# One core, fused attention and two dense blocks: a tile's scores begin one round later, and the next batch's v is fetched ten rounds later

## The chip, the cores and the metric

The kernel runs on one core of one Trainium2 chip. The metric is device time in microseconds of that core. Three runs of the kernel before took 867.61, 865.63 and 867.61 us, median 867.61. In what follows PE is the matrix engine (TensorE), PEld its weight loads, ACT the scalar engine, DVE the vector engine, POOL GpSimd, and SP the engine that issues the DMAs.

## What is computed

Attention with the heads mixed before and after the softmax, then two dense blocks. The change touches only the attention, for 4 batches, 12 heads, 448 rows and a head size of 64:

```python
scores = scale * np.matmul(q, k.transpose(0, 1, 3, 2))
scores = np.einsum('bhij,hg->bgij', scores, w_pre)      # mix heads
scores = scores - np.max(scores, axis=-1, keepdims=True)
attn = np.exp(scores)
attn = attn / (np.sum(attn, axis=-1, keepdims=True) + 1e-09)
attn = np.einsum('bhij,hg->bgij', attn, w_post)         # mix heads again
return np.matmul(attn, v)
```

Its result `x` goes through `_moe_ref` (a gated block with `w_in`, `w_sg`, `w_out`) and `_moe2_ref` (a block with `w_theta`, `w_tok_r`, `w_tok_i`, `w_ch`), which are left out here.

## The kernel before

**Tiles and rounds.** Each batch's 448 rows are cut into four tiles of 120, 120, 120 and 88 rows. A tile is worked off in rounds of two blocks of 10 rows (all 12 heads of 10 rows fill 120 partitions), so the four tiles of a batch have 6, 6, 6 and 5 rounds, 23 in a batch and 92 in all. Round r of the main loop is not one block's work from end to end but a slice of a software pipeline, written out by hand: `relayout(r + 4)`, `postmix(r)`, `premix(r + 2)` with its `rowmax` and `expo`, and parts of other tiles that tables of round numbers place there.

**The steps that matter.**

- `scores(b, t, c)` (L113 to L137): eight matmuls (L130) for the head pair c of a tile, into `psA`, a pool with one buffer (L66), then one ACT copy (L137) into the tile's `s`, a pool with two buffers (L61). A tile needs six of these, c = 0 to 5. So tile T's first copy writes the buffer of tile T - 2, and has to wait until all of that tile's relayouts have read it.
- `relayout(r)` (L142 to L148): two DMAs, SBUF to SBUF, that bring two blocks of `s` into `blk`, with heads on partitions.
- `premix(r)` (L150 to L156): eight matmuls from `blk` into two `psB` buffers, all there are of them (L74). `rowmax` (L162, DVE) and `expo` (L170, ACT) read them, so the premix of the next round can write them when these are done.
- `postmix(r)` (L192 to L207): 56 small matmuls (L201, L206), and two copies of the result into `at` (L218).
- `attn_v(b, t, c)` (L229 to L247): 20 matmuls (L242, L246) of the finished tile with v, six per tile, in the rounds of the tile after it.
- `load_k`, `load_q`, `load_v`: DMAs from SP. `vt` holds the v of two batches in turn.

**What sets the order.** Each engine works in the order in which the main loop writes instructions. In a round it is: relayout; the table `early` (DMAs); postmix; the copies into `at`; the tables `front` and `mid`; premix, rowmax, expo; the tables `work` and `late`. `units(T)` (L277) gives the rounds in which the six `scores` of tile T stand, spread evenly from `lo` to `hi`; the first in a round goes to `front` (ahead of the premix), a second one in the same round to `work` (after it, and before `attn_v`). `load_q` stands three rounds ahead of the first score, and the six `load_k` of the next batch stand in the rounds of the fourth tile's scores. `extra` is the decoding of a weight (L476 to L511) for the dense block, in steps on ACT, DVE and POOL in some of the rounds.

In what follows a round with no score is called an empty round, one with two scores a double round.

Of the kernel before, what the change touches and what calls it, by code (L numbers as in the profile page):

```python
# [28 lines left out]
LR, LQ = 4, 2  # L29
# [5 lines left out]
def attention(tc, nc, io, xT, B, extra, tail):  # L35
# [9 lines left out]
    tiles = [(b, t) for b in range(B) for t in range(len(TILES))]  # L45
    nt = len(tiles)
    first, last = {}, {}
# [4 lines left out]
    with ExitStack() as es:  # L52
# [219 lines left out]
        early, front, mid, work, late = {}, {}, {}, {}, {}  # L272

        def put(d, r, fn, *a):
            d.setdefault(r, []).append((fn, a))

        def units(T):  # L277
            lo, hi = first[tiles[T - 1]] - LR, first[tiles[T]] - LR - 1
            return [lo + (c * (hi - lo + 1)) // NP for c in range(NP)]

        for T in range(1, nt):
            b, t = tiles[T]
            u = units(T)
            for c in range(NP):
                put(front if u[c] not in u[:c] else work, u[c], scores, b, t, c)
            if T > 1:
                put(early, u[0] - QO, load_q, b, t)
            if t == 0:
                for c, r in enumerate(units(T - 1)):
                    put(early, r, load_k, b, c)  # L290
        for b in range(B):
            f = first[b, 0]
            for j in range(4):
                put(early, f - 14 + 3 * j if b else 1 + j, load_v, b, j)
        for T in range(nt):
            b, t = tiles[T]
            for c in range(NP):
# [815 lines left out]
def build(tc, nc, io, out):  # L1113
    with tc.manual_schedule(), ExitStack() as top:
        dram = top.enter_context(tc.tile_pool(name="scratch", bufs=1, space=bass.MemoryType.DRAM))
        xT = dram.tile([DM, B * S], F32, name="xT")
        x2T = dram.tile([DM, B * S], F32, name="x2T")
        d = Dense(tc, nc, io, xT, x2T, out)
        d.scratch(dram)
        right, left1, left2 = ExitStack(), ExitStack(), ExitStack()  # L1120
        tail, win_es, last_u, end = moe1(d, left1, right)
        th_es = moe2(d, left2, win_es, last_u, left1)
        for i in range(4):
            tail.setdefault(-2 + 2 * i, []).append(d.step)
        slots = top.enter_context(ExitStack())
        d.open_slots(slots)
        jobs = []
        for half, ks in ((1, range(KD)), (0, range(KE))):
            for k in ks:
                jobs += d.decode_tiles(io["w_in"], slice(128 * k, 128 * k + 128), HF * half, HF * half + HF,  # L1130
                                       lambda k=k, half=half: d.pieces(k, half))
        attention(tc, nc, io, xT, B, jobs, tail)
        while d.at < len(d.units):
            d.step()
        th_es.close()
        right.close()
        slots.close()
        left2.close()
# [69 lines left out]
```

## Time and profile before

| | |
|---|---|
| median of three runs | 867.61 us (865.63 to 867.61) |
| the profiled execution | 866.24 us |
| its span, first to last instruction | 864.5 us |
| attention: rounds 0 to 91 | 20 to 345 us of the span |
| PE busy | 842.7 us, 97% of the span |
| ACT busy | 493.6 us, 57% |
| DVE busy | 592.1 us, 68% |
| mean granted clock of PE | 0.996 of full speed |
| DMA moved | 142.16 MB, mean 164 GB/s |

A row of the timeline reads: start in us from the span's start, duration, engine, line, operation, result<-operands, shapes, count, and in brackets how long the engine was idle before it and what ended that. A row of the waits reads: who waited, for whom, us in total, times, longest. A row of the windows has, for one stretch, each engine's busy us, then the granted clock of PE (1.00 is 2.4 GHz, 0.50 is 1.2 GHz), the busy share of the DMA engines and GB/s. Matmuls overlap in the rows, so the time a step takes on PE is read from start to start. Line numbers are those of the kernel before.

### The profile page before, as it was taken

What the parts mean: (1) busy time and instruction counts of PE and PEld (TensorE: products, weight loads), DVE (VectorE), ACT (ScalarE), POOL (GpSimd) and SP (SyncE); (2) the same over time, 40 slices, a digit from 0 to 9 for tenths busy, and PEclk for the clock granted to TensorE, in tenths of its full rate; (3) what the DMA queues carried; (4) which work ended last, traced back from release to release, by engine and by line L of the source; (5) the groups of instructions that cost most, each with busy time, mean ns of one, the idle gap of its engine ahead of it and who ended that gap; (6) DMA issues with size and microseconds to landing.
All of it is one profiled execution on the core that took longest, in us unless ns stands there. A gap on an engine that the chain in (4) does not pass through costs nothing.

```text
span 864.5 us, 27167 instructions
## 1 busy us (share of the span) xinstructions
PE 842.7 (97%) x10984; PEld 664.9 (77%) x10984; DVE 592.1 (68%) x1364; ACT 493.6 (57%) x1106; POOL 204.6 (24%) x404
## 2 busy tenths in 40 slices
PE   7999999899989999999999999999999999999998
PEld 2465666466656666798988989898999999999997
DVE  5566676467666776879999998779784378338231
ACT  3688788579877886584845767247443155025010
POOL 0222223122222222000000000038228047306321
PEclk9999999899999999999999999999999999999999
DMA  5667657565776546551757867997611221300301
GB/s 195 212 223 227 196 180 229 179 201 172 249 202 209 177 158 167 153 159 50 247 180 240 270 196 230 351 299 230 214 38 45 83 54 31 118 19 1 118 11 64
DMA packets 108877, 142.16 MB, mean 164 GB/s; under 512 B 25680, under 2 KB 94800, under 8 KB 108752
## 3 DMA queue, kind: packets, MB, share of 16 engines
q1 hardware_dynamic: 108752, 140.42, 51.4%
q8 instruction: 87, 1.43, 0.7%
q14 instruction: 38, 0.31, 0.1%
HBM read 74.26 MB, written 27.59 MB: 118 GB/s over the span
## 4 chain that ended last, share of the span: by engine, by line
PE 91%; issue 3%; DMA 2%; DVE 2%; ACT 1%; POOL 0%; ACTq 0%; POOLq 0%; DVEq 0%; SPq 0%
PE ps L442 55%; PE psB L156 8%; PE psD L242 8%; PE psA L130 8%; PE psC L201 7%; PE psD L246 3%; DMA blk<-s 2%; PE psC L206 1%; PE ps L960 1%; DMA x<-x2T 1%; ACT s L137 0%; ACT e L170 0%; DVE s L134 0%; POOL x2s L438 0%; POOL z L438 0%
## 5 line engine op out<-in xcount | busy, mean ns | idle before, releaser
L170 ACT ACTIVATE e<-psB,nmx 128x448 f32<-128x448 f32 x180 | 112.3, 629 | 49.0 <-DVE nmx L162 47.3
L162 DVE TENSOR_REDUCE nmx<-psB 128x1 f32<-128x448 f32 x180 | 104.1, 619 | 27.9 <-PE psB L156 26.1
L442 PE MATMUL ps<-wtok,z 128*128 128x448 f32 x504 | 104.8, 368 | 0.0
L130 PE MATMUL psA<-k,q 64*64 64x448 f32 (+2 forms) x768 | 93.7, 547 | 10.1 <-ACT s L137 8.0
L242 PEld LDWEIGHTS psD<-at,v 128*64 128x64 f32 x1152 | 56.5, 137 | 60.6 <-issue 39.9
L442 PEld LDWEIGHTS ps<-wtok,z 128*128 128x128 f32 x504 | 94.6, 188 | 9.5
L156 PE MATMUL psB<-blk,kpre 64*64 64x448 f32 x720 | 97.9, 541 | 1.9 <-DMA blk<-s 1.1
L442 PE MATMUL ps<-wth,x2s 128*128 128x384 f32 x504 | 94.2, 342 | 2.4 <-POOL x2s L438 1.8
L137 ACT ACTIVATE s<-psA 124x896 f32<-124x896 f32 (+1 forms) x90 | 82.7, 919 | 24.0 <-PE psA L130 12.2
L438 POOL TENSOR_TENSOR x2s<-x,x2s 128x384 fp32r<-128x384 f32 x28 | 28.8, 1047 | 278.2 <-DMA xres<-xT 201.8
L442 PEld LDWEIGHTS ps<-wth,x2s 128*128 128x128 f32 x504 | 88.1, 188 | 4.1 <-POOL x2s L438 2.8
L442 PE MATMUL ps<-u,wch 128*128 128x448 f32 x432 | 89.9, 368 | 0.0
L442 PEld LDWEIGHTS ps<-u,wch 128*128 128x128 f32 x432 | 81.0, 188 | 8.1
L201 PE MATMUL psC<-wr,e 64*64 64x60 f32 x4320 | 83.4, 220 | 1.7 <-issue 1.1
L201 PEld LDWEIGHTS psC<-wr,e 64*64 64x64 f32 x4320 | 74.1, 136 | 8.6 <-POOL wr L188 5.3
L242 PE MATMUL psD<-at,v 128*64 128x120 f32 (+1 forms) x1152 | 77.3, 269 | 0.0
L438 POOL TENSOR_TENSOR z<-zz,z 128x384 fp32r<-128x384 f32 x56 | 63.8, 1159 | 56.4 <-ACT z L435 56.3
L435 ACT ACTIVATE u<-xres 128x448 fp32r<-128x448 f32 x24 | 13.8, 577 | 98.1 <-DVE xres L1021 98.1
L156 PEld LDWEIGHTS psB<-blk,kpre 64*64 64x64 f32 x720 | 36.7, 132 | 42.5 <-issue 19.3
L176 POOL TENSOR_SCALAR rc<-sum 128x2 f32<-128x2 f32 (+1 forms) x92 | 17.9, 195 | 210.5 <-ACT e L170 210.5
L188 POOL TENSOR_SCALAR wr<-wts,rc 128x60 f32<-128x60 f32 x180 | 54.1, 314 | 48.1 <-DVE rc L181 36.5
L442 PE MATMUL ps<-slot,x 128*128 128x512 f32 x252 | 60.1, 396 | 0.0
(111 smaller groups left out, 1437.6 us busy)
## 6 DMA issues: line engine op xcount, KB each, us to landing
blk<-s SPq DMA_DIRECT2D x176, 210.0 KB
draw<-in_w_in SPq DMA_DIRECT2D x24, 256.0 KB
k<-in_kvT SPq DMA_DIRECT2D x24, 224.0 KB
xraw<-xT SPq DMA_DIRECT2D x24, 224.0 KB
xres<-xT SPq DMA_DIRECT2D x24, 224.0 KB
x2T<-xres SPq DMA_DIRECT2D x24, 224.0 KB
xres<-x2T SPq DMA_DIRECT2D x24, 224.0 KB
out<-uu SPq DMA_DIRECT2D x24, 224.0 KB
```

Of the source, the lines that this page charges most:

```text
L130: nc.tensor.matmul(ps[e][r, :S], q[p, o + r.start:o + r.stop], k[p], start=True, stop=True)
L137: nc.scalar.activation(out=out, in_=pair[:m, :, :S], func=AF.Copy, scale=0.125)
L156: nc.tensor.matmul(ps[e][c:c + 64, :S], kpre[k, e], blk[k], start=True, stop=True)
L162: nc.vector.tensor_reduce(out=nmx[r][:, e:e + 1], in_=ps[:, :S], axis=AX.X, op=ALU.max, negate=True)
L170: nc.scalar.activation(out=x, in_=ps[:, :S], func=AF.Exp, bias=m[:, e:e + 1], accum_out=sm[:, e:e + 1])
L176: nc.gpsimd.tensor_scalar(out=rc[:, :m], in0=sm[:, :m], scalar1=1e-9, scalar2=1.0, op0=ALU.add, op1=ALU.mult)
L188: nc.gpsimd.tensor_scalar(out=w, in0=wts, scalar1=rc[:, e:e + 1], scalar2=0.0, op0=ALU.mult, op1=ALU.add)
L201: nc.tensor.matmul(pc[r][h][c:c + 64, o:o + H], x[p, 128 * jc + c:128 * jc + c + 64], w[p], start=(e == 0 and jc == 0), stop=(not two and ...
L242: nc.tensor.matmul(ps[p], v[:, jc, p], main[:, H * jc + 2 * c + i], start=(o == 0 and jc == 0), stop=False)
L246: nc.tensor.matmul(px[p] if e else ps[p, 0], v[q, 3, p], rest[q, 2 * c + i], start=(o == 0 and e == 1), stop=(o > TI))
L438: eng.tensor_tensor(out=out, in0=in_, in1=hi.bitcast(F32), op=ALU.subtract)
L442: self.nc.tensor.matmul(ps, l, r, start=(i == 0), stop=(i == len(terms) - 1))
```

## The change

```diff
         def units(T):
-            lo, hi = first[tiles[T - 1]] - LR, first[tiles[T]] - LR - 1
+            lo, hi = first[tiles[T - 1]] - LR + (T > 1), first[tiles[T]] - LR - 1
             return [lo + (c * (hi - lo + 1)) // NP for c in range(NP)]
...
             for j in range(4):
-                put(early, f - 14 + 3 * j if b else 1 + j, load_v, b, j)
+                put(early, f - 3 + 2 * j if b else 1 + j, load_v, b, j)
```

`lo` moves one round later from tile 2 on, `hi` stays. Where the tile before has six rounds, six scores stood in six rounds, 1 1 1 1 1 1, and now stand as 0 2 1 1 1 1. Where it has five (the first tile of batches 1, 2 and 3), they stood as 2 1 1 1 1 and now stand as 0 2 1 2 1. `load_q`, and the `load_k` of a batch's end, move with them. The four parts of the next batch's v stood 14, 11, 8 and 5 rounds before the batch's first round f, and now stand at f - 3, f - 1, f + 1 and f + 3; the first `attn_v` that reads it is in round f + 6.

On PE, round 38 (in batch 1's last tiles; the scores are those of the first tile of batch 2) was

```order
L206 MATMUL psC<-wr,e 64x60 x4
L130 MATMUL psA<-k,q 64x448 x2
L130 MATMUL psA<-k,q 60x448 x2
L156 MATMUL psB<-blk_136,kpre 64x448
L156 MATMUL psB<-blk_137,kpre 64x448
L156 MATMUL psB<-blk_136,kpre 64x448
L156 MATMUL psB<-blk_137,kpre 64x448
L242 MATMUL psD<-at,v 64x2x12x5 x6
```

from the end of its postmix to the start of its attn_v. In the changed kernel the same round, on PE, is

```order
L206 MATMUL psC<-wr,e 64x60 x4
L130 MATMUL psA<-k,q 64x448 x2
L130 MATMUL psA<-k,q 60x448 x2
L156 MATMUL psB<-blk_136,kpre 64x448
L156 MATMUL psB<-blk_137,kpre 64x448
L156 MATMUL psB<-blk_136,kpre 64x448
L156 MATMUL psB<-blk_137,kpre 64x448
L130 MATMUL psA<-k,q 64x448 x2
L130 MATMUL psA<-k,q 60x448 x2
L242 MATMUL psD<-at,v 64x2x12x5 x6
```

A second score now stands behind the premix and ahead of attn_v; before, this was so one round earlier, in round 37, which now has no score.

On ACT, rounds 37 and 38 (`at` is the copy after the postmix, `s` the copy of a score, `e` the two exponentials, `dp`, `dl` and `slot` belong to the decoding) were

```order
L218 COPY at<-psC 128x84x5
L137 ACTIVATE s<-psA 124x896
L484 ACTIVATE dp<-draw 128x256
L485 ACTIVATE dl<-draw 128x256
L170 ACTIVATE e,sum<-psB,nmx 128x448 x2
L137 ACTIVATE s<-psA 124x896
L218 COPY at<-psC 128x84x5
L137 ACTIVATE s<-psA 124x896
L500 ACTIVATE slot<-da 128x256
L170 ACTIVATE e,sum<-psB,nmx 128x448 x2
```

and the same two rounds on ACT, with the first row of the next one, are now

```order
L218 COPY at<-psC 128x84x5
L484 ACTIVATE dp<-draw 128x256
L485 ACTIVATE dl<-draw 128x256
L170 ACTIVATE e,sum<-psB,nmx 128x448 x2
L218 COPY at<-psC 128x84x5
L137 ACTIVATE s<-psA 124x896
L500 ACTIVATE slot<-da 128x256
L170 ACTIVATE e,sum<-psB,nmx 128x448 x2
L137 ACTIVATE s<-psA 124x896
L218 COPY at<-psC 128x84x5
```

The copy of a double round's second score stands behind both exponentials. Each tile from tile 2 on now has such a place.

On SP, the DMAs of rounds 35 to 37 (the `blk` are relayouts) were

```order
L96 DMA k<-in_kvT 128x448
L108 DMA v<-in_vN 128x768
L476 DMA draw<-in_w_in 128x512
L148 DMA blk_136<-s 120x1x448
L148 DMA blk_137<-s 120x1x448
L96 DMA k<-in_kvT 128x448
L269 DMA xT<-x 128x3x120
L148 DMA blk_138<-s 120x1x448
L148 DMA blk_139<-s 120x1x448
```

and on SP the same stretch is now

```order
L96 DMA k<-in_kvT 128x448
L476 DMA draw<-in_w_in 128x512
L148 DMA blk_136<-s 120x1x448
L148 DMA blk_137<-s 120x1x448
L96 DMA k<-in_kvT 128x448
L269 DMA xT<-x 128x3x120
L148 DMA blk_138<-s 120x1x448
L148 DMA blk_139<-s 120x1x448
```

The part of v that stood ahead of round 36's relayout (`blk_136`, `blk_137`, the last that reads the `s` of the tile two before) is gone from there.

## Rows read from the trace of the kernel before

**Rows 1.** The page: PE's busy time, share of the span and instructions

```profile
PE 842.7 (97%) x10984; PEld 664.9 (77%) x10984; DVE 592.1 (68%) x1364; ACT 493.6 (57%) x1106; POOL 204.6 (24%) x404
```

**Rows 2.** Waits of the attention stage: waiter <- releaser, total, times, longest

```profile
ACT s L137 <- DMA blk<-s: 8.9, 5, 4.1
```

**Rows 3.** Timeline, rounds 61 and 62: score, its copy, first exponential, next score

```profile
246.00 0.94 PE L130 MATMUL psA<-k,q 64*64 64x448 f32 x8
...
247.01 0.92 ACT L137 ACTIVATE s<-psA 124x896 f32<-124x896 f32 x1 [0.22 <-PE psA L130]
...
248.49 0.63 ACT L170 ACTIVATE e<-psB,nmx 128x448 f32<-128x448 f32 x1 [0.56 <-DVE nmx L162]
...
249.37 0.94 PE L130 MATMUL psA<-k,q 64*64 64x448 f32 x8
```

**Rows 4.** Timeline, round 60, a double round: the two scores and their copies

```profile
239.49 0.94 PE L130 MATMUL psA<-k,q 64*64 64x448 f32 x8
...
242.38 0.92 ACT L137 ACTIVATE s<-psA 124x896 f32<-124x896 f32 x1 [1.96 <-DMA blk<-s]
...
243.35 0.20 PEld L130 LDWEIGHTS psA<-k,q 64*64 64x64 f32 x8 [2.95 <-ACT s L137]
...
243.50 0.63 ACT L170 ACTIVATE e<-psB,nmx 128x448 f32<-128x448 f32 x1
...
244.72 0.92 ACT L137 ACTIVATE s<-psA 124x896 f32<-124x896 f32 x1
```

**Rows 5.** Timeline, first scores of rounds 14 (a double round) and 15

```profile
71.99 0.93 PE L130 MATMUL psA<-k,q 64*64 64x448 f32 x8
...
77.63 0.93 PE L130 MATMUL psA<-k,q 64*64 64x448 f32 x8
```

**Rows 6.** Timeline, round 37 (double), its second score, first scores of 38 and 39

```profile
153.07 0.94 PE L130 MATMUL psA<-k,q 64*64 64x448 f32 x8
...
159.01 0.29 PEld L130 LDWEIGHTS psA<-k,q 64*64 64x64 f32 x8 [5.03 <-ACT s L137]
...
163.86 1.28 PE L130 MATMUL psA<-k,q 64*64 64x448 f32 x8
...
167.57 0.93 PE L130 MATMUL psA<-k,q 64*64 64x448 f32 x8
```

**Rows 7.** Window of round 37, after its second score

```profile
161.00:162.00 1.00, 1.00 (x12) 0.80 (x8) 0.00 (x0) 0.77 (x1) 0.11 (x1) 0.50 0.83 282
```

**Rows 8.** Timeline of SP: a part of v, and the relayouts of rounds 36 and 37

```profile
147.53 0.63 SPq L108 DMA_DIRECT2D v<-in_vN  x1
...
149.41 1.69 SPq L148 DMA_DIRECT2D blk<-s  x2
...
153.19 4.40 SPq L148 DMA_DIRECT2D blk<-s  x4
```

**Rows 9.** Windows while those were under way, and of the scoreless rounds at the end

```profile
148.00:150.00 2.00, 2.00 (x75) 1.46 (x77) 0.76 (x3) 1.84 (x6) 0.36 (x2) 1.00 0.98 302
...
320.00:342.00 22.00, 22.00 (x619) 13.60 (x611) 14.04 (x33) 12.36 (x36) 5.56 (x21) 1.00 0.57 152
```

**Rows 10.** The chain that ended last, round 62: start, us, PE's score

```profile
249.54 0.76 PE psA L130 x8
```

**Rows 11.** Timeline, rounds of the last tile, which have no score: premix to premix

```profile
323.76 1.47 PE L156 MATMUL psB<-blk,kpre 64*64 64x448 f32 x8
...
324.26 0.20 PEld L156 LDWEIGHTS psB<-blk,kpre 64*64 64x64 f32 x6 [0.36 <-ACT e L170]
...
326.91 1.48 PE L156 MATMUL psB<-blk,kpre 64*64 64x448 f32 x8
```

**Rows 12.** Timeline, scores of two rounds beside attn_v of an 88-row tile

```profile
199.41 0.94 PE L130 MATMUL psA<-k,q 64*64 64x448 f32 x8
...
202.62 0.94 PE L130 MATMUL psA<-k,q 64*64 64x448 f32 x8
```

**Rows 13.** Timeline, round 43: a gap of PE with no releaser

```profile
181.71 0.26 PE L201 MATMUL psC<-wr,e 64*64 64x60 f32 x1 [0.64 <-issue]
```

## The prediction

> **What bounds the kernel now.** I read the page first: PE is busy 97% of the span and no other engine comes near [rows 1]. So time goes where PE stands still, and an edit to the attention is priced by what it does to PE's round. Then the waits of the attention stage: ACT's copy of a score waited for relayout DMAs 8.9 us in 5 cases, the longest 4.1 [rows 2]. The long ones lie in the double rounds 14, 37 and 60, where a new batch's scores begin, and there PE's second score waits for the copy. Then the timeline of an undisturbed round: from score to score 3.37 us (246.00 to 249.37) [rows 3], and round after round repeats this, with PE going from one step to the next. There is no slack on PE that could take up a new wait.
>
> **What the change removes: the three DMA waits.** The first copy of tile T waits for the last relayout of tile T - 2, written one round earlier. To price the wait I need a double round without it. In the ordinary round the copy starts 1.01 us after the score (247.01 after 246.00) [rows 3]. In round 60 the second score starts 0.97 after the copy's start (243.35 after 242.38) [rows 4]. So the second score could start 1.98 after the first. From there PE needs 2.65 (243.35 to 246.00) to the next round's score [rows 3, 4], which is 4.63 in all. The next score also needs psA free again: the first exponential starts 2.49 after the score (248.49 after 246.00) [rows 3], the second score's copy stands behind both exponentials and starts 1.22 later (244.72 after 243.50) [rows 4], and the score may follow 0.97 after that, together 4.68. The later of the two holds: a clean double round takes 4.68 from its first score to the next round's.
>
> Measured: round 60 took 6.51 (239.49 to 246.00) [rows 3, 4], so 1.83 to gain. Round 14 took 5.64 (71.99 to 77.63) [rows 5], 0.96 to gain. Round 37 took 10.79 (153.07 to 163.86), and round 38 another 3.71 (to 167.57) [rows 6]. In that stretch PE's granted clock had dropped to 0.50, the 1.2 GHz level [rows 7], after the weight loads of PE had stood still for 5.03 us [rows 6]. That gives 10.79 - 4.68 + 3.71 - 3.37 = 6.45. Together 9.24 us.
>
> I take all of it as gained, since the first copy now comes two rounds after that relayout instead of one. The empty round in between lasts about 3.15 us (below), against a longest wait of 4.1 [rows 2]. The missing 1 us is covered by v: a part of it was issued at 147.53, ahead of the relayout at 149.41 [rows 8]. It has 384 KB (128 x 768 elements of 4 bytes), which at the 302 GB/s of that stretch [rows 9] is an estimated 1.3 us of queue.
>
> **What it adds: 14 more double rounds and 14 empty ones.** Tiles 2 to 15 each get an empty round ahead of their first score and one more double round (at a batch's start there were already 2 1 1 1 1, now 0 2 1 2 1). The scores, copies and matmuls are the same in number. What counts is what two scores in one round cost, and whether the empty round gives it back.
>
> A double round costs 4.68 - 3.37 = 1.31 over an ordinary one. Only 0.76 of it is the score [rows 10]; the rest is PE waiting for the single psA.
>
> An empty round does not shrink by a score. The rounds of the last tile show it, since they have no score at all: premix to premix is 3.15 (323.76 to 326.91), and the premix's second half waits there for the exponential of the round before (0.36 idle at 324.26), because psB has only two buffers [rows 11]. So an empty round gives back 3.37 - 3.15 = 0.22, not 0.76. Where attn_v is that of an 88-row tile an ordinary round takes 3.21 (199.41 to 202.62) [rows 12]. There a double round costs 4.68 - 3.21 = 1.47, because psA sets it, and the empty one gives back 0.06. Of the 14 pairs 3 fall there (the empty rounds 25, 48 and 71), and I put tile 2's pair, in rounds 2 and 3 before attn_v begins, with them.
>
> The sum: 10 x (1.31 - 0.22) + 4 x (1.47 - 0.06) = 10.9 + 5.6 = 16.5 us added.
>
> **What I cost at nothing.** The DMAs that move: k and q keep their distance to their first use within a round. v's last part is now issued in round f + 3 and needed in f + 6, three rounds or 10.1 us; the slowest landing I find is a relayout issued at 149.41 [rows 8] whose reader, ACT's copy in round 37, came 4.1 late [rows 2]: after 153.07 [rows 6] plus the 1.01 of the score, at about 158.1, so 8.7 us. That hides v with 1.4 to spare. Behind a late v only attn_v waits, but with it all of PE. SP itself is passed by v at four places a batch, and the relayouts there have two rounds before their premix. The Trainium skill, DMA: Bandwidth & Descriptors, Rules for kernel authors, advises to issue a DMA early and wait for it late, which speaks against moving v; by that rule the 1.4 us is what is left of the cover, and no run here shows v arriving late. The decoding's ACT steps in some double rounds push the exponentials by a few tenths, up to 1 us in all. PE also has gaps with no releaser, such as 0.64 in round 43 [rows 13]; they come where DMA is busiest, and may grow or shrink as v moves, by 2 us either way. These go into the range.
>
> So 16.5 - 9.2 = +7.3 us. On the profiled execution's 866.24 us that is 873.5. The median of the runs is 867.61, 1.4 above that execution, which would give 874.9; I say **874**.
>
> **Rivals.**
> 1. *Faster: the pairs cost nothing.* If two rounds with 0 and 2 scores take as long as two with 1 each, only the gain is left: 866.24 - 9.2 = 857. It decides at PE: faster by 0.3% (2.6 us, about what a measurement of this kernel can tell from no change) needs a pair under (9.2 - 2.6) / 14 = 0.47 us, where I have 1.1 to 1.4. For it: ACT is busy 57% only [rows 1]. Against it: the 0.36 at the premix without scores [rows 11], and the second score's 1.98 with one psA [rows 3, 4]. 15%.
> 2. *No change: only half of it costs.* If the empty round gives the whole score back (0.76), or the double costs no more than its score, a pair costs some 0.55: 14 x 0.55 = 7.7, less 9.2, gives 865. 17%.
> 3. *The waits stay*, because relayouts of a busy queue land yet later: 866.24 + 16.5 = 883. The removed v speaks against it. 4%.
> 4. *The clock falls more often.* A fall made the stretch from second score to next score 4.85 (159.01 to 163.86) [rows 6] instead of 2.65, and the next round 0.34 longer: 2.5 us each, 36 for 14, so 902. Against it: the scoreless rounds pause in each round [rows 11] at a granted clock of 1.00 [rows 9]. The Trainium skill, TensorE: Matmul & The Clock Gate, A second HAM failure mode: psum-queue depth-cycling, says that short idling of PE between matmul groups, from cycling through PSUM, can make its clock swing; in the scoreless rounds the trace does not agree. 2%.
>
> That the change doesn't do what it says is excluded by the order of instructions, which shows the second score behind the premix.
>
> **How the numbers follow.** The forecast, 10 to 21 us added and 7 to 12 removed, has the remaining 62%; its own range is 866 to 882. To the low side I reach to the middle of rival 2, so the range is 865 to 882. Slower by over 0.3%: the forecast's 62% and rivals 3 and 4, 68%, less 1 for the forecast's low edge: 67%. Within 0.3%: 18%. Faster: 15%.
>
> **What would show it.** Right: no wait of a score's copy for a relayout over 0.5 us at rounds 15, 38 and 61; PE's granted clock at 1.00 through 150 to 170 us; double rounds of 4.6 to 4.8 in which a score waits some 0.4 for the copy, 17 of them; empty rounds near 3.15 in which the premix waits for the exponential; the attention ending some 7 us later than at 345. Wrong: double rounds near 4.1 or empty rounds near 2.6 (rival 1 or 2), an attn_v that waits for v, or waits for relayouts at other places.

## The result, and the profile after

The changed kernel takes 872.78 us (median of six runs, 870.57 to 874.78), the kernel before 867.61 beside it (six runs, 865.63 to 870.59). The ratio is 1.0064, with a 95% interval of 1.0038 to 1.0091: slower, by 5.2 us. The profiled execution has a span of 870.1 us (864.5 before) and a mean granted clock of 0.999 (0.996 before).

The page of the kernel after, PE's busy time and its share of the span, then the other engines:

```profile
PE 850.6 (98%) x10984; PEld 661.9 (76%) x10984; DVE 592.2 (68%) x1364; ACT 493.9 (57%) x1106; POOL 204.6 (24%) x404
```

The counts of instructions are those of [rows 1] on every engine: nothing was added or taken away, only the order is another.

The waits of the kernel after, 0 to 352 us, each row who waited, for whom, us in total, times, longest:

```profile
PEld psA L130 <- ACT s L137: 22.9, 25, 1.2
PEld psB L156 <- ACT e L170: 16.7, 39, 1.5
PE psA L130 <- ACT s L137: 6.4, 20, 1.0
...
ACT s L137 <- DMA blk<-s: 0.2, 1, 0.2
```

The first three of these rows in the kernel before, same window:

```profile
PEld psA L130 <- ACT s L137: 13.9, 7, 5.0
PEld psB L156 <- ACT e L170: 12.6, 30, 1.5
PE psA L130 <- ACT s L137: 8.0, 4, 4.3
```

The last row of the kernel after answers to [rows 2]: of 8.9 us in 5 cases, 0.2 in one is left. The first and third show what came in its place, a score that waits for the copy of the one before it: where there were a few long waits (up to 5.0 us) there are now many short ones. The weight loads stand for 0.9 us on average (22.9 in 25), the matmuls for 0.3 (6.4 in 20). The wait that the edit is about is gone, and a small one stands in every double round.

The timeline of rounds 31 to 33 of the kernel after, an empty round, a double round and the one behind it (columns as in [rows 3]):

```profile
135.70 0.88 PE L201 MATMUL psC<-wr,e 64*64 64x60 f32 x48
...
137.01 0.20 PEld L156 LDWEIGHTS psB<-blk,kpre 64*64 64x64 f32 x6 [0.35 <-ACT e L170]
...
138.85 0.88 PE L201 MATMUL psC<-wr,e 64*64 64x60 f32 x48
...
139.66 0.93 PE L130 MATMUL psA<-k,q 64*64 64x448 f32 x8
...
140.67 0.92 ACT L137 ACTIVATE s<-psA 112x896 f32<-112x896 f32 x1
...
141.64 0.97 PE L130 MATMUL psA<-k,q 64*64 64x448 f32 x8 [0.29 <-ACT s L137]
142.15 0.63 ACT L170 ACTIVATE e<-psB,nmx 128x448 f32<-128x448 f32 x1 [0.56 <-DVE nmx L162]
...
143.38 0.91 ACT L137 ACTIVATE s<-psA 112x896 f32<-112x896 f32 x1
...
143.47 0.88 PE L201 MATMUL psC<-wr,e 64*64 64x60 f32 x48
...
144.34 0.97 PE L130 MATMUL psA<-k,q 64*64 64x448 f32 x8
...
146.93 0.88 PE L201 MATMUL psC<-wr,e 64*64 64x60 f32 x48
```

From postmix to postmix (L201) the empty round takes 3.15 us, the double round 4.62 and the one behind it 3.46. All three took 3.36 to 3.43 before. In the double round the chain is to be read as the prediction built it: score at 139.66, its copy 1.01 later, the second score 0.97 after that, then both exponentials on ACT ahead of the second copy (143.38), and the next score only 0.96 behind its start. From score to score that is 4.68 (139.66 to 144.34). In the empty round the second half of the premix stands for 0.35 us until ACT has read psB.

The windows of the kernel after, where [rows 7] showed the lower clock (columns as there: the granted clock is the third number from the end):

```profile
150.00:172.00 22.00, 21.42 (x552) 12.46 (x548) 15.10 (x37) 17.52 (x40) 6.21 (x20) 1.00 0.65 198
```

**The attention, round by round.** Both kernels were also profiled a second and a third time (experiment 9 below). The stage from the first postmix to the last can then be cut in three: the sum of the shortest length that each round has in the three profiles of its kernel (rounds 14, 37 and 60 of the kernel before, which wait for relayouts in each profile, are put in as double rounds without a wait, 4.63, and rounds 15 and 38 as 3.36); what those five rounds took over that; and what all other rounds took over their shortest, which I call gaps.

| profile | stage, us | rounds alone | waits for relayouts | gaps |
|---|---|---|---|---|
| before, first | 323.40 | 310.31 | 9.38 | 3.71 |
| before, second | 319.60 | 310.31 | 6.24 | 3.05 |
| before, third | 325.83 | 310.31 | 10.20 | 5.32 |
| after, first | 328.16 | 327.67 | 0 | 0.49 |
| after, second | 328.08 | 327.67 | 0 | 0.41 |
| after, third | 329.29 | 327.67 | 0 | 1.62 |

By the means the change adds 17.36 us of round, and takes away 8.61 of wait and 3.19 of gaps: +5.56, beside 5.2 in the medians of the runs.

A gap that a round has in all three profiles counts as round in this table. Round 43 of the kernel before never took under 3.89 and round 54 never under 3.70, while both take 3.36 in experiment 4. With these two put at 3.36, the change adds 18.2 us of round and takes away 4.1 of gaps; the net is the same.

### The profile page after: what moved, and what is told of

Read it like the earlier page. It is cut to its first block, busy times and chain, and to the rows that moved or that the text cites. A ratio compares the mean times of both kernels' runs of the same rounds, so it can differ in the third digit from the quotient of the medians.

```text
span 870.1 us, 27112 instructions
## 1 busy us (share of the span) xinstructions
PE 850.6 (98%) x10984; PEld 661.9 (76%) x10984; DVE 592.2 (68%) x1364; ACT 493.9 (57%) x1106; POOL 204.6 (24%) x404
## 4 chain that ended last, share of the span: by engine, by line
PE 81%; DVE 6%; ACT 5%; issue 4%; DMA 4%; POOL 0%; SPq 0%; ACTq 0%; DVEq 0%; POOLq 0%
PE ps L442 48%; PE psB L156 8%; PE psA L130 7%; PE psD L242 7%; PE psC L201 6%; PE psD L246 3%; ACT s L137 2%; DMA x2T<-xres 2%; DMA blk<-s 1%; ACT e L170 1%; PE psC L206 1%; DVE nmx L162 1%; PE ps L960 1%; DVE r L975 1%; DVE r L974 1%
## 5 line engine op out<-in xcount | busy, mean ns | idle before, releaser
L156 PE MATMUL psB<-blk,kpre 64*64 64x448 f32 x720 | 103.3, 544 | 2.4 <-DMA blk<-s 1.2
L201 PE MATMUL psC<-wr,e 64*64 64x60 f32 x4320 | 81.2, 219 | 0.5
L201 PEld LDWEIGHTS psC<-wr,e 64*64 64x64 f32 x4320 | 72.7, 135 | 6.3 <-POOL wr L188 4.0
L156 PEld LDWEIGHTS psB<-blk,kpre 64*64 64x64 f32 x720 | 34.4, 132 | 43.8 <-issue 20.0
```

Source lines behind the costliest of these rows:

```text
L156: nc.tensor.matmul(ps[e][c:c + 64, :S], kpre[k, e], blk[k], start=True, stop=True)
L201: nc.tensor.matmul(pc[r][h][c:c + 64, o:o + H], x[p, 128 * jc + c:128 * jc + c + 64], w[p], start=(e == 0 and jc == 0), stop=(not two and ...
```

## The experiments

**1. v alone.** Is the score shift needed for the waits to go? The units keep their place.

```diff
-                put(early, f - 14 + 3 * j if b else 1 + j, load_v, b, j)
+                put(early, f - 3 + 2 * j if b else 1 + j, load_v, b, j)
```

> Only v is fetched later; the scores stand as in the kernel before. Theory A (the copies wait because they come one round after the relayout; v only lengthens the queue by about 1.3 us a part): rounds 14, 37 and 60 still wait for a relayout, each about 1.3 us less than the 1.1, 4.1 and 2.0 of before, and the clock may no longer fall in round 37, so 3 to 6 us faster, about 863. Rival B (v ahead of the relayout is the whole cause): no such wait is left, about 9 us faster, 858. Rival C (v plays no part): 867.6, the same waits.

Measured: 860.36 us (858.16 to 864.16), ratio 0.9918 [0.9889, 0.9947]. The waits of this kernel, and the windows at 144 us of this kernel and of the kernel before:

```profile
ACT s L137 <- DMA blk<-s: 2.0, 5, 0.6
```

```profile
144.00:152.00 8.00, 8.00 (x201) 4.72 (x193) 5.85 (x15) 6.87 (x17) 3.06 (x10) 1.00 0.83 267
```

```profile
144.00:152.00 8.00, 8.00 (x196) 4.89 (x193) 5.54 (x14) 5.84 (x14) 2.36 (x7) 1.00 0.96 262
```

Round 37 of this kernel, from its first postmix to that of round 38:

```profile
152.93 0.88 PE L201 MATMUL psC<-wr,e 64*64 64x60 f32 x48
...
157.89 0.88 PE L201 MATMUL psC<-wr,e 64*64 64x60 f32 x48
```

Round 14 took 4.63, round 37 took 4.96 and round 60 took 5.20, with the clock at 1.00: 0.9 us of wait are left in the rounds of the 8.6. In this stretch the DMA engines were busy 96% in the kernel before and 83% here, at about the same GB/s. So they were all but full there, and with v moved they no longer were. Moving v by itself does nearly all that the change does for the waits, and the score shift is left with little to gain.

**2. The scores alone.** v stays early.

```diff
-            lo, hi = first[tiles[T - 1]] - LR, first[tiles[T]] - LR - 1
+            lo, hi = first[tiles[T - 1]] - LR + (T > 1), first[tiles[T]] - LR - 1
```

> Only the scores stand one round later; v is fetched as in the kernel before. Theory A: 17 double rounds of 4.6, 14 empty ones of 3.15, waits for relayouts under 1 us at rounds 15, 38 and 61, so nearly the time of the whole change, 872 to 874. Rival B: the waits stay as long as v stands in front, 880 or more.

Measured: 876.0 us (874.3 to 878.99), ratio 1.0099 [1.0067, 1.013], some 2 us above what theory A expected. Most double rounds take 4.63 and most empty ones 3.15, as in the kernel after. The wait for relayouts is down to the same single row of 0.2 us:

```profile
ACT s L137 <- DMA blk<-s: 0.2, 1, 0.2
```

So either edit removes the waits, v alone all but 0.9 us of them, and both together remove them once. The pairs' cost is paid in full here.

**3. The shift at the batch starts only,** where the waits were, with v later.

```diff
-            lo, hi = first[tiles[T - 1]] - LR, first[tiles[T]] - LR - 1
+            lo, hi = first[tiles[T - 1]] - LR + (tiles[T][1] == 0), first[tiles[T]] - LR - 1
```

> v later, and the scores later only for the first tile of batches 1, 2 and 3, where the long waits were. Theory A: 3 pairs of an empty and a double round at 1.1 us each, 3.5 in all, against 9.2 us of waits removed: about 862, 5 to 8 us faster than before. Rival (the pairs don't cost, something else made the whole change slower): the same gain as with all tiles moved, that is no gain, 870 to 873.

Measured: 862.39 us (859.85 to 865.86), ratio 0.9944 [0.9917, 0.997]. Rounds 14 and 15 take 3.14 and 4.63, rounds 60 and 61 take 3.15 and 4.68. The stage takes 318.09 (its first postmix is at 21.16, its last at 339.25), 10.1 less than in the kernel after; this profile has gaps of 1.24, 0.84 and 0.6 us in rounds 24, 47 and 72. With these set aside it is 12.8 us for the 11 tiles that aren't shifted here, 1.2 a tile.

**4. A third buffer for `s`,** in the order of before: what the copy waits for is taken away without moving anything. To make room, k has six buffers and is fetched a round later, q two, e four.

```diff
-        s_p = pool_r("a_s", 2)
-        k_p = pool_r("a_k", NP + 3)
-        q_p = pool_r("a_q", 3)
+        s_p = pool_r("a_s", 3)
+        k_p = pool_r("a_k", NP)
+        q_p = pool_r("a_q", 2)
...
-        e_p = pool("a_e", 6)
+        e_p = pool("a_e", 4)
...
-                    put(early, r, load_k, b, c)
+                    put(early, r + 1, load_k, b, c)
```

> The order of the scores and of v is that of the kernel before, but s has three buffers instead of two, so a tile's first copy waits for relayouts six rounds older (to make room: 6 buffers of k instead of 9 with k fetched one round later, 2 of q instead of 3, 4 of e instead of 6). Theory A: no wait of a copy for a relayout anywhere, clock 1.00 throughout, no further empty or double rounds: 9 us faster, about 858.5. Rival (the relayout's queue would stall PE at the next place, the premix that reads blk): waits of the premix for relayouts appear in rounds 14 to 16, 37 to 39 and 60 to 62, and less than half of the 9 us is gained.

Measured: 859.38 us (858.29 to 860.02), ratio 0.9889 [0.9845, 0.9933]. The waits have no row for a copy of a score behind a relayout, and round 37 takes 4.63:

```profile
152.27 0.88 PE L201 MATMUL psC<-wr,e 64*64 64x60 f32 x48
...
156.90 0.22 PE L201 MATMUL psC<-wr,e 64*64 64x60 f32 x1
```

So the wait was for the buffer. It cost the kernel before some 7 us by the medians (866.35 beside it) and 9.6 by the ratio; that the smaller pools of k, q and e and the later k play no part in this is not shown.

**5. Both remedies,** the third buffer and v later.

```diff
-        s_p = pool_r("a_s", 2)
+        s_p = pool_r("a_s", 3)
...
-                put(early, f - 14 + 3 * j if b else 1 + j, load_v, b, j)
+                put(early, f - 3 + 2 * j if b else 1 + j, load_v, b, j)
```

(k, q and e are as in experiment 4.)

> Three buffers of s as before, and v fetched later too. Theory: the two edits take away the same waits, so together they give no more than 1 us over either alone: 858 to 860. Rival (each takes away a part of its own, such as PE's gaps without a releaser where DMA is busy): 855 or less.

Measured: 857.39 us (856.17 to 859.73), ratio 0.9888 [0.9849, 0.9927]. It can't be told from experiments 1 and 4 by their intervals. The two remedies take away the same wait and don't add up. Any of the three is faster than both kernels of this case, by about 1% of the kernel before.

**6. One part of v.** Does a part of v cost the waits its own 1.3 us of queue, as the prediction had it, or more?

```diff
-                put(early, f - 14 + 3 * j if b else 1 + j, load_v, b, j)
+                put(early, (f - 3 if j == 1 else f - 14 + 3 * j) if b else 1 + j, load_v, b, j)
```

> The kernel before, with one of v's four parts moved: the one 11 rounds ahead of a batch, which stands just ahead of the relayout that the copy waits for, goes to 3 rounds ahead; the other three stay. Theory A, as v alone has shown it with all parts (wait 0.6 at most): this part alone does it, waits under 1 us at rounds 14, 37 and 60 and a clock of 1.00, about 860. Rival (the whole queue of the rounds before counts): about half of the 4.1 us wait stays in round 37, and 862 to 865.

Measured: 861.51 us (858.63 to 867.13), ratio 0.9948 [0.9921, 0.9974], between the kernel before and experiment 1, whose interval it overlaps. The profiled execution is the slowest of the ten of this kernel:

```profile
ACT s L137 <- DMA blk<-s: 5.5, 4, 3.1
```

```profile
150.00:172.00 22.00, 18.74 (x466) 12.07 (x468) 11.68 (x28) 14.48 (x34) 4.07 (x14) 0.92 0.61 184
```

Here the wait in round 37 still lasts 3.1 us and the clock still falls. This execution also has a gap that has nothing to do with the waits: in round 65 PE stood still for 2.5 us with no releaser, the granted clock was 0.53 over the 2 us behind it, and the round took 4.5 us longer than its kind.

```profile
259.85 0.38 PE L201 MATMUL psC<-wr,e 64*64 64x60 f32 x10 [2.53 <-issue]
...
260.00:262.00 2.00, 2.00 (x31) 1.34 (x30) 0.60 (x1) 0.56 (x1) 0.00 (x0) 0.53 0.90 266
```

By the runs one part of four is worth 4.5 us (by the ratio; 6.2 by the medians). The mean granted clock of each run points the same way: it is 0.998 or more in 8 of these 10 runs, in 3 of the 25 of the kernel before beside them, and in 8 of the 9 of experiment 1. So in most runs the one part spares most of the fall of the clock; in the one that was profiled it doesn't remove the wait.

**7. Half the copy in double rounds.** Is the double round as long as the prediction says because psA has one buffer, so that the copies stand in PE's way?

```diff
-                nc.scalar.activation(out=out, in_=pair[:m, :, :S], func=AF.Copy, scale=0.125)
+                w = S // 2 if (b, t, c) in twice else S
+                if w < S:
+                    nc.gpsimd.memset(out[:, :, w:], 0.0)
+                nc.scalar.activation(out=out[:, :, :w], in_=pair[:m, :, :w], func=AF.Copy, scale=0.125)
```

> The changed kernel, but in the 17 double rounds ACT copies only the first half of each score's columns and POOL writes zeros in the other half (half of those scores is left out). Theory: PE's second score waits for the first one's copy, so with a copy shorter by about 0.4 us the double round falls from 4.63 to 4.2 or 4.25 and the round behind it from 3.46 to 3.37, together about 8 us, about 865. Rival (a double round is long because of its matmuls, not the wait): double rounds stay at 4.6, 872 to 873.

Measured: 868.09 us (864.73 to 870.99), ratio to the kernel before 1.001 [0.9988, 1.0031], so 4.7 below the kernel after. The same double round, its lines now those of this kernel (L204 is the postmix, L140 the copy):

```profile
136.89 0.88 PE L204 MATMUL psC<-wr,e 64*64 64x60 f32 x48
...
138.71 0.55 ACT L140 ACTIVATE s<-psA 112x448 f32<-112x448 f32 x1
...
139.31 0.20 PEld L130 LDWEIGHTS psA<-k,q 64*64 64x64 f32 x8 [0.69 <-ACT s L140]
...
141.14 0.88 PE L204 MATMUL psC<-wr,e 64*64 64x60 f32 x48
```

The copy takes 0.55 instead of 0.92, and the double round 4.25 instead of 4.62: the 0.37 comes back whole, in 15 of the 17 double rounds (0.13 and 0.29 in rounds 49 and 61). So the copy sets the length of the double round. That is 6 us of the stage; gaps of 1.6 and 0.5 us in rounds 65 and 24 of this profile take 2 of it back. The round behind didn't fall to 3.37 as expected but stayed at 3.46. There the second copy, though shorter, still ends (141.96) just ahead of the next score:

```profile
141.42 0.54 ACT L140 ACTIVATE s<-psA 112x448 f32<-112x448 f32 x1
...
142.02 0.97 PE L130 MATMUL psA<-k,q 64*64 64x448 f32 x8
```

**8. Half the exponentials ahead of an empty round.** Is it psB that keeps the empty round from shrinking?

```diff
-                nc.scalar.activation(out=x, in_=ps[:, :S], func=AF.Exp, bias=m[:, e:e + 1], accum_out=sm[:, e:e + 1])
+                w = S // 2 if r in short else S
+                if w < S:
+                    nc.gpsimd.memset(x[:, w:], 0.0)
+                nc.scalar.activation(out=x[:, :w], in_=ps[:, :w], func=AF.Exp, bias=m[:, e:e + 1], accum_out=sm[:, e:e + 1])
```

> The changed kernel, but in the 14 rounds ahead of an empty one ACT takes the exponentials of only the first half of the columns and POOL writes zeros in the other half (half of those exponentials is left out). Theory: the premix of an empty round waits for psB, which these exponentials hold, so the empty rounds fall from 3.15 to about 2.6 and the time by 6 to 8 us, about 866. Rival (some other engine's chain sets 3.15): empty rounds stay at 3.15, 872 to 873.

Measured: 871.0 us (868.14 to 874.61), ratio to the kernel before 1.0033 [1.0008, 1.0058]. The same empty round (L204 is the postmix, L173 the exponential):

```profile
134.53 0.45 ACT L173 ACTIVATE e<-psB,nmx 128x224 f32<-128x224 f32 x1 [0.23 <-DVE nmx L162]
...
134.62 0.88 PE L204 MATMUL psC<-wr,e 64*64 64x60 f32 x48
...
135.38 0.47 PEld L156 LDWEIGHTS psB<-blk,kpre 64*64 64x64 f32 x8
...
137.49 0.88 PE L204 MATMUL psC<-wr,e 64*64 64x60 f32 x48
```

With exponentials of 0.45 instead of 0.63 us the premix waits for nothing, and the empty round takes 2.87 instead of 3.15. Of the 14 empty rounds 13 are shorter by 0.27 to 0.30 (a gap hides it in round 65). The mechanism holds in the rounds: 3.7 us of the stage, half of the 6 to 8 expected, since a round without that wait takes 2.87 and not 2.6. The time moved by 1.8 us only, which is inside what the runs of the two kernels scatter; in the profile, gaps in rounds 9, 38 and 65 (0.4, 0.54 and 0.9 us) make up for the rest.

**9. The same kernels again.** In the first profiles the kernel before had gaps in six rounds (I had overlooked a seventh, 0.50 in round 9), and the kernel after in none worth naming. Do they belong to the order of the instructions, or to chance? The two kernels, unchanged, two more profiles each.

> The kernel before, unchanged, profiled a second time. In its first profile PE has six rounds that are longer than their kind without any wait for another engine: rounds 13 (0.56 us), 20 (0.43), 36 (0.81), 43 (0.96), 54 (0.56) and 76 (0.51), 3.83 us in all. Theory A, the gaps belong to this order of instructions: the same six rounds are again longer by about the same, 3.5 to 4.2 us in all. Theory B, the gaps fall where chance puts them in each execution: other rounds are longer, and the sum lies anywhere between 1 and 6 us. The waits of the score copies for relayouts (9 us) and the long rounds 14, 37 and 60 are expected as before by both.

> The changed kernel, unchanged, profiled a second time. In its first profile no round of the attention is longer than its kind. Theory A, the gaps belong to the order of instructions: again none, first to last postmix 328.1 to 328.4 us. Theory B, they fall where chance puts them: some rounds are longer, by 0.3 to 1.6 us each and up to 5 us in all, so 328 to 333 us.

> The kernel before, a third time. Theory A: the same six rounds longer, 3.5 to 4.2 us in all. Theory B: other rounds than in the first two profiles, and another sum.

> The changed kernel, a third time. Theory A: no longer rounds, 328.1 to 328.4 us from first to last postmix. Theory B: a sum that differs from that of the first two profiles.

Measured: 862.95 and 867.92 us for the kernel before, 870.41 and 871.5 for the kernel after. These are single runs, and one more of the kernel before beside them, without a profile, took 871.7, so they don't rank the two kernels. The table above has the stages. The gaps of the kernel before aren't in the same six rounds: round 43 is longer in all three profiles, 20 in the first two, 76 in the first and the third, 54 more in the third, 64 in the third alone, 36 in the first alone. Rows of PE in the postmix (L201) of rounds 43 and 64 of the third profile, which answer to [rows 13]:

```profile
181.47 0.26 PE L201 MATMUL psC<-wr,e 64*64 64x60 f32 x1 [0.22 <-issue]
...
257.42 0.85 PE L201 MATMUL psC<-wr,e 64*64 64x60 f32 x42 [0.87 <-issue]
```

So the size of one gap changes from execution to execution. But the sums of the two kernels don't overlap (3.05 to 5.32, and 0.41 to 1.62), so neither theory holds as it stood. The waits scatter more than I had thought: in the third profile of the kernel before the long one lies in round 14 (9.86 us, the clock at 0.75 over 70 to 82 us) and not in round 37 (6.35):

```profile
70.00:82.00 12.00, 8.00 (x176) 5.00 (x176) 4.22 (x11) 5.00 (x12) 1.89 (x6) 0.75 0.77 218
```

## Why the prediction came out as it did

The forecast was 874 and slower; the median is 872.78. The net is +5.2 where the sum gave +7.3. The terms have to be taken one by one: the mechanism of the two large ones is borne out and each is off by under 2 us, the gaps were missed by 3 to 4, and since these errors partly cancel, that the time came so near to 874 is in part luck.

- **The waits removed: 9.24 forecast, 8.61 measured** as the mean of three profiles, 9.38 in the one that was read. All of it went, as forecast, with the clock at 1.00 through 150 to 172 us. But the size was read from one execution, and the three lie between 6.24 and 10.20.
- **What removes them.** I put v at one part and 1.3 us, worked out from 384 KB at 302 GB/s [rows 8, 9], as the missing microsecond behind an empty round. This step was mis-sized: v alone took all but 0.9 us of the wait (experiment 1). The row that should have told it was there, a DMA share of 0.98 in [rows 9]: with the engines all but full, v ahead of a relayout pushes it back (how much one part does is open, experiment 6), and a wait that is cut short also spares the fall of the clock, some 2.5 of the 6.45 us of rounds 37 and 38 by the prediction's own figures (rival 4). Nor did the shift need v for the missing microsecond: with v early it left 0.2 us of wait by itself (experiment 2). For the forecast of this change it made no difference, since both edits were made.
- **The pairs: 16.5 forecast, 17.4 to 18.2 measured.** The double round of 4.68 from score to score is exact, for the reason given (experiment 7). Most empty rounds take 3.13 to 3.17, as the last tile's rows had shown [rows 11], for the reason given (experiment 8). What I left out is the round behind the double one: it starts with the second copy still on ACT, and takes 0.10 longer beside an attn_v of 120 rows and 0.25 to 0.29 beside one of 88. In return the double rounds there take 4.48, not the 4.68 that I charged. Rounds 31 to 33 are 1.15 longer than three ordinary ones (1.09 forecast), rounds 25 to 27 are 1.50 longer (1.41 forecast).
- **The gaps: put at nothing, with 2 us either way; measured -3.2 to -4.1.** This is the term that failed, and it is more than the difference between +7.3 and +5.2. I had [rows 13] in front of me and counted it once, where the round lengths would have shown 3.7 us of such gaps in the stage. Nor do the gaps come where DMA is busiest, as the prediction has it: around that of [rows 13] the DMA share was 0.62, and over the attention (20 to 345 us) 0.64. What they are stands in the last section.

```profile
178.00:182.00 4.00, 3.36 (x96) 2.23 (x92) 2.69 (x7) 2.77 (x9) 0.79 (x3) 1.00 0.62 181
```

- **What I cost at nothing.** No attn_v waits for v in any of the three profiles of the kernel after. Outside the stage the first profiles differ by some 0.85 us, half of it ahead of the first postmix and half behind the last, which isn't explained.
- **The rivals.** Rival 1 (pairs cost nothing) and rival 2 (half of it) are out: a pair costs 1.1 to 1.5 us in the rounds, and 1.2 in experiment 3. Rival 3 is out by the 0.2 us of wait left. Rival 4 is out as well: PE stops for a moment in each of the 17 double and most of the empty rounds, at a granted clock of 0.999 over the span. The Trainium skill, TensorE: Matmul & The Clock Gate, A second HAM failure mode: psum-queue depth-cycling, says that the clock can swing under short stops between groups of matmuls; this trace doesn't show it.

**What stays open** is why the sum of the gaps shrinks as far as it does. One profile each of the scores' shift alone has about 2.8 us of gaps in its stage (experiment 2) and of v alone about 3.3 (experiment 1), and experiments 7 and 8, which are the kernel after with a little less ACT work, have 2 to 3 us of them. Three profiles of a kernel tell that the difference is there. The last section shows what a gap is and gives a lead on why there are fewer; no run here settles it.

## What to carry to other kernels

Before a step is moved to make room for a late transfer, look at what else is in the DMA queue ahead of that transfer: here a load whose reader was 17 rounds away was in front, and moving v alone was worth 0.8%, while the score shift that was meant to help cost some 17 us of rounds. Before work is gathered into fewer rounds, look at the PSUM buffers: here an empty and a double round cost 1.1 to 1.5 us more than two ordinary ones, because the wait for the single psA sets the double round and the wait for the two psB keeps the empty one from shrinking. And where a sum is made from one profile, compare every round with its kind first, so that gaps without a releaser are counted, and take a second profile for waits that come from a full queue.

## What the runs showed of the hardware

**Here late was better than early, where the DMA engines were full.** The Trainium skill, DMA: Bandwidth & Descriptors, Rules for kernel authors, has transfers issued early. In the kernel before, the parts of v were issued 11 to 20 rounds ahead of their first reader; issued 8 to 11 rounds later, 3 to 9 rounds ahead of it, they never came late, and the kernel took 0.9918 of its time (experiment 1).

**PE's gaps without a releaser stand where a new block of its instructions begins.** The page of the kernel after shows instruction fetches as a DMA queue of their own:

```profile
q8 instruction: 87, 1.43, 0.7%
```

In the traces each of these 87 packets has 16 KB, and PE has 22343 instructions in the kernel before, so a packet is worth 256 of them. A round has 92 matmuls and as many weight loads on PE, so a new block begins every 1.4 rounds. Counted through in the attention (24 to 350 us) of all 14 profiles, 48 matmuls stood for over 0.1 us without a releaser, and all 48 are at one place of a block of 256 (remainder 193 or 194, counted from the first PE instruction in the trace). In each of the 48 the packet that belongs there had landed only 1.27 to 1.69 us before. At the 732 of the 913 block starts where it had landed 1.7 us before or earlier, there is no such stop. That of [rows 13] is one of the 48: its packet landed at 180.21 and the matmul started at 181.71. Round 36 of the same profile, longer by 0.81, has its stop on a weight load, 1.49 us behind a packet that landed at 148.94:

```profile
150.43 0.19 PEld L156 LDWEIGHTS psB<-blk,kpre 64*64 64x64 f32 x3 [0.63 <-issue]
```

Of the gaps of whole rounds nearly all are of this kind: in the profiles of the two kernels and of experiments 1, 2, 4, 5 and 6, 56 rounds (14, 15, 37, 38, 60 and 61, where the waits lie, left aside) are over 0.25 us longer than the shortest of their kind, and 55 of them hold a block start whose packet had landed less than 1.7 us before. So PE waited there for its own instructions. No run changed the fetches; it is the place and the time of the stops that show it.

The Trainium skill, Runtime: NRT & Kernel Launch, Instruction fetch mechanics, says that they are fetched by DMA in blocks of 256 while earlier ones run, and that the cost of crossing a block is mostly hidden. The trace agrees on the blocks; hidden it was at most block starts, and the rest cost the kernel before 3 to 5 us in 320.

This gives a lead on why the gaps shrink. Block starts whose packet had landed less than 1.7 us before number 15, 14 and 19 in the three profiles of the kernel before, and 5, 9 and 10 in those of the kernel after; they number 7 in experiment 2, which shifts the scores alone, and 11 in experiment 1, which moves v alone. A block takes PE 4.8 us in the kernel before (the median) and 5.1 in the kernel after, so a fetch has more time there. That this is the reason is argued, and why a fetch comes late in one execution and not in the next isn't shown.
